# Fewer warm-up products, an earlier LayerNorm tile, and a later weight load on another queue, in a gated mix of linear attention and an MLP mixer

## The chip, the cores and the metric

One core of one Trainium2 chip. The metric is the device time of one execution in microseconds (us), lower is better. "Span" is the time from the first to the last instruction of a profiled execution; it is mostly about 1.7 us shorter than that execution's device time (264.9 against 266.56 us for the profiled run of the kernel before).

Engines by their names in the profile: PE (TensorE matmul), PEld (its weight loads), DVE (VectorE), ACT (ScalarE), POOL (GpSimd), SP (SyncE, used here only to issue DMAs). All times inside an execution count from the start of its span. PE writes its products into PSUM banks (`pp` in the profile); "evacuation" is the copy of a result out of PSUM by another engine. The "clock record" is the trace's list of the stretches in which PE was granted full or half rate.

## The reference, cut to what matters

The input x has 2048 rows of 640. The kernel computes `g*a + (1-g)*b`: g is a sigmoid gate, a is a linear attention with 32 heads of 20, b is a mixer block with two LayerNorms.

```python
def _A_ref(x, wqkv, wo):
    ...                                   # q, k, v per head; phi(t) = t+1 if t > 0 else exp(t), + 1e-6
    kv  = jnp.einsum("bhsd,bhse->bhde", pk, v)
    z   = jnp.einsum("bhsd->bhd", pk)
    num = jnp.einsum("bhqd,bhde->bhqe", pq, kv)
    den = jnp.einsum("bhqd,bhd->bhq", pq, z)[..., None] + 1e-6
    return (num / den) ... @ wo

def _B_ref(x, w1, w2, w3, w4):
    h  = _gelu(_layernorm(x) @ w1)        # LN1
    hs = (four column groups of h, each shifted by 1 or 2 rows) @ w2
    x1 = x + hs
    return x1 + _gelu(_layernorm(x1) @ w3) @ w4      # LN2
```

## The kernel before

Tiles of 512 rows (four) are worked on in chunks of 128 rows (sixteen). The order on each engine is the order of the source text. All PSUM results go through one pool of four pairs of banks, taken in turn.

The start: x's first chunk is loaded and transposed on PE; the other chunks come transposed by DMA. PE is kept busy with products of ones until data is there.

```python
    warmup(6)                # 6 products of 512 columns
    warmup(3, P)             # 3 of 128 columns
    ...                      # 5 PE transposes of x's first chunk (L211), 1 of the gate vector
    warmup(3, P)
    for dc in range(DC):     # 5 slices of the contraction
        k_mm(kp, 0, (dc,))   # K of chunk 0 (L190), 2 products
        if dc < DC - 1:
            warmup(1, 2 * P)
    k_evac(kp, 0)
    for c in range(1, NCH):  # K of chunks 1 to 15
        ...
```

The middle. `ln1_apply(c)` normalises a chunk on DVE into one of four buffers and has the SP queue transpose it by DMA into `lnxT`:

```python
    def ln1_apply(c):
        ...
        lnx = work.tile([P, D], BF16, name="ln")              # pool "work": bufs=4
        nc.vector.tensor_scalar(lnx[:], x_sb[:, c, 0:D], ...) # L297
        nc.sync.dma_start_transpose(lnxT[t][...], lnx[:])     # L299

    def den_evac(pt):        # 1 / den
        nc.scalar.activation(pt[:, 1, :], pt[:, 0, :], ACT.Copy, bias=1e-6)
        ...
            nc.vector.reciprocal(r_bf[:], pt[:, 1, :])        # L254, reads a PSUM pair

    ...
    for cc in range(CPT):
        ln1_apply(2 * CPT + cc)            # LN1 tile 2
    ...
    for fcs in w1_split:
        w1_unit(0, fcs)
    kv_unit()
    den_evac(den_mm())
    for fcs in w1_split:
        w1_unit(1, fcs)
    for cc in range(CPT):
        ln1_apply(3 * CPT + cc)            # LN1 tile 3, the last
    s1.close()
    ...
    nc.gpsimd.dma_start(w4_sb[:, 0:FF, :], ...)      # w4, 2080 KB, and two pieces of 80 KB
    nc.gpsimd.dma_start(w4_sb[0:FR, FF, :], ...)
    nc.gpsimd.dma_start(w4_sb[FR:P, FF, :], ...)
    ...
    for j in range(DC):
        m_unit(j)            # five output-weight units on PE (L379), each copied out by ACT (L381)
    r_unit()                 # spreads the reciprocals over the rows (L259)
    ...                      # W2 (L415), LN2 of tile 0, w1_unit(2), w1_unit(3), then W3 and W4 by tile
```

## Time and profile before

| | before |
|---|---|
| device time, median (range) of the first four runs | 267.24 us (266.69 to 267.68) |
| span of the profiled execution | 264.9 us |
| PE busy | 260.5 us |
| first PE product, first K product, first K product of chunk 1 | 0.83, 4.83, 7.20 us |
| first W2 product | 88.28 us |
| start of the last PE product, and from there to the end | 261.13 us, 3.73 us |

The page of the kernel before, its line of busy times and the head of its chain of waits:

```profile
...
PE 260.5 (98%) x1744; PEld 162.6 (61%) x1744; DVE 139.6 (53%) x270; ACT 84.3 (32%) x122; POOL 22.7 (9%) x58
...
PE 97%; ACT 1%; DVE 0%; issue 0%
...
```

PE is busy practically all of the time and is the chain. So engines other than PE matter only where PE waits for them, and by the start times of PE's products there is just one such place of any size: around `r_unit`, ahead of the first W2 product, the starts are 467 ns apart, where other products of 512 columns, as the row-broadcast's are, follow each other after 216.

The start, from the timeline (start in us, length in us, engine, line, what, count, and in brackets the idle time before it and what ended it):

```profile
...
0.83 3.04 PE L202 MATMUL pp<-const-bfloat16-1.0 128*128 128x512 bf16 x9 [0.83 <-PEq L574]
...
3.67 0.42 PE L211 MATMUL pp<-ident,x_sb 128*128 128x128 bf16 x2
...
4.83 0.74 PE L190 MATMUL pp<-wk_sb,xT 128*128 128x320 bf16 x2
...
5.58 0.64 PE L190 MATMUL pp<-wk_sb,xT 128*128 128x320 bf16 x2
...
6.16 0.44 PE L190 MATMUL pp<-wk_sb,xT 128*128 128x320 bf16 x2
...
```

PE begins at half rate: two K products at 4.83 and 5.09 start 267 ns apart, later ones 136. The trace's clock record has full rate from 5.99 us on. x's first chunk landed at 3.10 us, but nine warm-ups stand ahead of its transposes.

The middle, from the timeline:

```profile
...
78.98 1.39 POOL L396 DMA_DIRECT2D w_sb<-in_B_w_dram  x1 [5.29 <-PE pp L360]
...
80.25 3.36 DVE L254 RECIPROCAL r_bf<-pp 128x512 bf16<-128x512 f32 x1
...
84.97 2.90 PE L379 MATMUL pp<-wo_sb,kvT 128*32 128x320 bf16 x80
...
85.74 3.08 ACT L381 CAST m_sb<-pp 128x640 bf16<-128x640 f32 x5
86.92 1.16 DVE L297 TENSOR_SCALAR ln<-x_sb,mv,rstd 128x640 bf16<-128x640 bf16 x3
...
87.80 0.40 PE L259 MATMUL pp<-r_bf,emat 32*128 32x512 bf16 x4
...
88.28 5.59 PE L415 MATMUL pp<-w_sb,hsT 128*128 128x320 bf16 x40
88.28 0.45 DVE L297 TENSOR_SCALAR ln<-x_sb,mv,rstd 128x640 bf16<-128x640 bf16 x1 [0.20 <-DMA lnxT<-ln]
...
```

The reciprocal (L254) runs directly behind the kv evacuation (the copies into `kvT`, which end at 80.19 us). w4's load is issued from POOL at 78.98 us. The last LN1 tile is normalised (L297, 3 + 1) at 86.9 to 88.7 us, and the fourth of these waits for a transpose: its buffer still held LN1 tile 2, whose fourth transpose was issued at 79.58 us. That one, by source line:

```profile
...
L299 SPq DMA_TRANSPOSE lnxT<-ln x1: 1227/1227/1227, 79.6 to 79.6; - x1
...
DMA to landing us min/median/max: 8.6/8.6/8.6
```

It took 8.6 us from issue to landing; lone ones take 2.6. In that time w4's 2240 KB were on the way.

### The profile page before, as it was taken

The numbers are of one execution on the slowest core, as the hardware profiler recorded it, in microseconds if no ns is written. First come the engines' busy times: TensorE is split into PE (matmuls) and PEld (weight loads), VectorE is DVE, ScalarE is ACT, GpSimd is POOL, SyncE is SP. The second block draws the span as 40 slices with busy tenths as digits, with TensorE's granted clock in tenths as the row PEclk, the third lists the DMA queues.
The fourth block names the chain that finished last, engine by engine and source line by source line (L and its number), as shares of the span: only waits on it lengthen the run. The fifth ranks groups of instructions, "written<-read, shape, count | busy, mean of one in ns | idle before, by whom it ended". The sixth has DMA issues, their size and how long they took to land.

```text
span 264.9 us, 4267 instructions
## 1 busy us (share of the span) xinstructions
PE 260.5 (98%) x1744; PEld 162.6 (61%) x1744; DVE 139.6 (53%) x270; ACT 84.3 (32%) x122; POOL 22.7 (9%) x58
## 2 busy tenths in 40 slices
PE   8999999999999999999999999999999999999994
PEld 4777555788754644555666556567555566455663
DVE  1688778899856797955412364503464413122132
ACT  1555544321165635622420313330222340333100
POOL 7100010012223140001000001000001000000000
PEclk9999999999999999999999999999999999999999
DMA  7999989015668952000132000042000042000011
GB/s 194 148 182 350 369 293 330 9 33 121 125 97 217 228 105 52 0 0 2 25 74 77 25 0 2 11 88 77 25 0 2 1 99 74 27 0 2 0 50 50
DMA packets 44749, 23.62 MB, mean 89 GB/s; under 512 B 35450, under 2 KB 43642, under 8 KB 44730
## 3 DMA queue, kind: packets, MB, share of 16 engines
q1 hardware_dynamic: 43792, 20.57, 32.6%
q0 software_dynamic: 496, 2.29, 2.9%
q10 hardware_dynamic: 442, 0.49, 0.5%
q8 instruction: 13, 0.21, 0.3%
q14 instruction: 6, 0.05, 0.1%
HBM read 12.21 MB, written 2.62 MB: 56 GB/s over the span
## 4 chain that ended last, share of the span: by engine, by line
PE 97%; ACT 1%; DVE 0%; issue 0%
PE pp L479 22%; PE pp L462 21%; PE pp L190 8%; PE pp L307 8%; PE pp L415 8%; PE pp L446 8%; PE pp L341 8%; PE pp L232 8%; PE pp L202 2%; PE pp L467 1%; PE pp L488 1%; ACT m_sb L381 1%; PE pp L360 1%; PE pp L247 0%; PE pp L379 0%; PE pp L211 0%
## 5 line engine op out<-in xcount | busy, mean ns | idle before, releaser
L470 ACT ACTIVATE h<-pp 128x1024 bf16<-128x1024 f32 (+1 forms) x28 | 27.8, 993 | 102.8 <-PE pp L462 94.4
L462 PE MATMUL pp<-lnxT,w_sb 128*128 128x512 bf16 x260 | 60.4, 379 | 0.0
L479 PE MATMUL pp<-w_sb,h 128*128 128x320 bf16 x416 | 57.9, 299 | 0.0
L479 PEld LDWEIGHTS <-h 128*128 128x128 bf16 x416 | 40.0, 98 | 17.0 <-issue 1.9
L462 PEld LDWEIGHTS <-w_sb 128*128 128x128 bf16 x260 | 25.5, 98 | 26.7
L495 DVE SCALAR_TENSOR_TENSOR oc<-pp,omg,x 128x640 bf16<-128x640 f32 x15 | 12.9, 882 | 44.0 <-PE pp L488 27.1
L449 DVE SCALAR_TENSOR_TENSOR x<-pp,gate,x 128x640 f32<-128x640 f32 x16 | 13.9, 868 | 29.4 <-PE pp L446 29.4
L182 ACT ACTIVATE e<-pp 128x640 bf16<-128x640 f32 (+1 forms) x26 | 21.5, 827 | 9.6 <-PE pp L232 9.6
L446 PE MATMUL pp<-m_sb,pqT 128*128 128x320 bf16 x160 | 24.3, 299 | 0.0
L418 DVE TENSOR_TENSOR x<-pp,x_sb 128x640 f32<-128x640 f32 x16 | 13.1, 820 | 20.7 <-PE pp L415 20.7
L415 PE MATMUL pp<-w_sb,hsT 128*128 128x320 bf16 x160 | 23.9, 299 | 0.1
L190 PE MATMUL pp<-wk_sb,xT 128*128 128x320 bf16 (+1 forms) x160 | 23.0, 303 | 0.0
L307 PE MATMUL pp<-x_sb,pk 128*128 128x320 bf16 (+1 forms) x160 | 22.3, 300 | 0.0
L232 PE MATMUL pp<-xT,hsT 128*128 128x512 bf16 x100 | 21.7, 379 | 0.0
L307 PEld LDWEIGHTS <-pk 128*128 128x128 bf16 x160 | 18.8, 117 | 3.5
L415 PEld LDWEIGHTS <-hsT 128*128 128x128 bf16 x160 | 15.6, 98 | 8.2 <-issue 0.2
L446 PEld LDWEIGHTS <-pqT 128*128 128x128 bf16 x160 | 15.7, 98 | 7.7
L190 PEld LDWEIGHTS <-xT 128*128 128x128 bf16 x160 | 15.8, 99 | 6.1
L341 PE MATMUL pp<-lnxT,w_sb 128*128 128x512 bf16 x80 | 17.9, 379 | 0.0
L232 PEld LDWEIGHTS <-hsT 128*128 128x128 bf16 x100 | 11.8, 118 | 9.7
L277 POOL TENSOR_SCALAR rstd<-mv 128x4 f32<-128x4 f32 (+1 forms) x11 | 3.5, 318 | 147.5 <-DVE mv L283 147.5
L184 DVE SCALAR_TENSOR_TENSOR pk<-pp,e 128x640 bf16<-128x640 f32 x16 | 13.2, 825 | 1.7
(79 smaller groups left out, 192.9 us busy)
## 6 DMA issues: line engine op xcount, KB each, us to landing
out_dram<-oc SPq DMA_DIRECT2D x15, 160.0 KB, 1.8
w_sb<-in_B_w_dram SPq DMA_DIRECT2D x1, 2160.0 KB, 8.5
w_sb<-in_B_w_dram POOLq DMA_DIRECT2D x1, 2080.0 KB, 12.7
x_sb<-in_A_x_dram SPq DMA_DIRECT2D x2, 640.0 KB, 9.8
x_sb<-in_A_x_dram SPq DMA_DIRECT2D x1, 1120.0 KB, 8.5
wo_sb<-in_A_wo_dram SPq DMA_DIRECT2D x6, 160.0 KB, 9.2
hsT<-in_A_wqkv_dram SPq DMA_DIRECT2D x1, 800.0 KB, 6.0
m_sb<-in_A_wqkv_dram SPq DMA_DIRECT2D x1, 800.0 KB, 11.0
```

Source lines behind the costliest of these rows:

```text
L182: nc.scalar.activation(ev, src, ACT.Exp)
L184: nc.vector.scalar_tensor_tensor(dst, src, 0.0, ev, op0=ALU.max, op1=ALU.add)
L190: nc.tensor.matmul(pt[:, hf, 0:n], lhsT=xT[:, dc, c * P:(c + 1) * P], rhs=wk_sb[:, dc, hf * HD:hf * HD + n], start=(dc == 0), stop=(dc == ...
L232: nc.tensor.matmul(pt[:, t % 2, :], lhsT=wq_sb[:, dc, :].rearrange("p (m j) -> p j m", j=DC)[:, j], rhs=xT[:, dc, t * TS:(t + 1) * TS], st ...
L307: nc.tensor.matmul(pt[:, hf, 0:HD + hf], lhsT=w, rhs=x_sb[:, c, hf * HD:(hf + 1) * HD + hf], start=(c == 0), stop=(c == NCH - 1))
L341: nc.tensor.matmul(pt[:, i, :], lhsT=w, rhs=lnxT[t][:, dc, :], start=(dc == 0), stop=(dc == DC - 1))
L415: nc.tensor.matmul(pt[:, hf, 0:HD], lhsT=hsT[:, fc, 2 + c * P:2 + (c + 1) * P], rhs=w2_sb[:, fc, hf * HD:(hf + 1) * HD], start=(fc == 0), ...
L446: nc.tensor.matmul(pt[:, hf, 0:HD], lhsT=pqT[:, j, c * P:(c + 1) * P], rhs=m_sb[:, j, hf * HD:(hf + 1) * HD], start=(j == 0), stop=(j == D ...
L449: nc.vector.scalar_tensor_tensor(x1, pt[:, :, 0:HD], gate[:, c:c + 1], x1, op0=ALU.mult, op1=ALU.add)
L462: nc.tensor.matmul(pt[:, k, :], lhsT=w3_sb[:, dc, fc * P:(fc + 1) * P], rhs=lnT[:, dc, :], start=(dc == 0), stop=(dc == DC - 1))
L470: nc.scalar.activation(h2[:, 2 * i * TS:2 * i * TS + n], pt[:].rearrange("p h e -> p (h e)")[:, 0:n], ACT.Gelu_apprx_tanh)
L479: nc.tensor.matmul(dst, lhsT=st[t]["h2"][:, fc * TS + cc * P:fc * TS + (cc + 1) * P], rhs=w4_sb[:, fc, a:b], start=start and fc == 0, stop ...
```

## The change

Intent: let x's first chunk have its turn as soon as it has landed (part 1); put the normalisation of the last LN1 tile ahead of the reciprocal of den (part 2); and take w4's load out of the way of the transposes, onto the SP queue behind LN2 of tile 0 (part 3).

```diff
@@ part 1
-    def k_mm(pt, c, dcs, hfs=(0, 1), last=DC - 1):
+    def k_mm(pt, c, dcs, first=0):
...                                          (start flag on dc == first)
-    warmup(6)
-    warmup(3, P)
+    warmup(5)
+    warmup(1, P)
...
-    warmup(3, P)
-    for dc in range(DC):
-        k_mm(kp, 0, (dc,))
-        if dc < DC - 1:
+    warmup(5, P)
+    for n, dc in enumerate((1, 0, 2, 3, 4)):
+        k_mm(kp, 0, (dc,), first=1)
+        if n < DC - 1:
             warmup(1, 2 * P)
@@ part 2
     kv_unit()
+    for cc in range(CPT):
+        ln1_apply(3 * CPT + cc)
     den_evac(den_mm())
     for fcs in w1_split:
         w1_unit(1, fcs)
-    for cc in range(CPT):
-        ln1_apply(3 * CPT + cc)
     s1.close()
@@ part 3
-    nc.gpsimd.dma_start(w4_sb[:, 0:FF, :], ...)      (and the two small pieces)
...
     for fcs in w1_split:
         w1_unit(2, fcs)
         if fcs[0] == 0:
             ln2_apply(0, CPT - 1)
+    nc.sync.dma_start(w4_sb[:, 0:FF, :], ...)        (and the two small pieces)
     scale_t(0)
```

More of the change, by code (lines that the diff above doesn't have):

```diff
@@ L184, in phi @@
         nc.vector.scalar_tensor_tensor(dst, src, 0.0, ev, op0=ALU.max, op1=ALU.add)
-    def k_mm(pt, c, dcs, hfs=(0, 1), last=DC - 1):
+    def k_mm(pt, c, dcs, first=0):
         for dc in dcs:
-            for hf in hfs:
+            for hf in range(2):
                 n = HD + hf
                 nc.tensor.matmul(pt[:, hf, 0:n], lhsT=xT[:, dc, c * P:(c + 1) * P],
-                                 rhs=wk_sb[:, dc, hf * HD:hf * HD + n], start=(dc == 0), stop=(dc == last))
+                                 rhs=wk_sb[:, dc, hf * HD:hf * HD + n], start=(dc == first), stop=(dc == DC - 1))
     def k_evac(pt, c):
@@ L395 @@
     w4_sb = w4p.tile([P, FF + 1, D], BF16)
-    nc.gpsimd.dma_start(w4_sb[:, 0:FF, :], B_w4[0:FF * P, :].rearrange("(c p) f -> p c f", p=P))
-    nc.gpsimd.dma_start(w4_sb[0:FR, FF, :], B_w4[FF * P:F, :])
-    nc.gpsimd.dma_start(w4_sb[FR:P, FF, :], B_w4[FF * P:F, :])
     h2p = ctx.enter_context(tc.tile_pool(name="h2p", bufs=1))
@@ L538 @@
             ln2_apply(0, CPT - 1)
+    nc.sync.dma_start(w4_sb[:, 0:FF, :], B_w4[0:FF * P, :].rearrange("(c p) f -> p c f", p=P))
+    nc.sync.dma_start(w4_sb[0:FR, FF, :], B_w4[FF * P:F, :])
+    nc.sync.dma_start(w4_sb[FR:P, FF, :], B_w4[FF * P:F, :])
     scale_t(0)
```

## The prediction

> **What bounds the kernel.** TensorE. Page section 1: PE busy 260.5 of 264.9 us; the chain of waits is 97% PE. By start times PE pauses only for 0.83 us at the start, about 0.3 us near 88 us, and 3.4 us after the last product. Only work removed from PE's queue, or PE's waits, can count.
>
> **Part 1, warm-ups.** PE runs at half rate first: 512-column warm-ups start 427 ns apart, and 320-column products go from 267 to 136 ns apart at about 6.0 us. The Trainium skill ("TensorE: Matmul & The Clock Gate", Part 1) says that the clock is released by time of activity, not by a count of products; so I take the release to stay at 6.0 us. x's first chunk lands at 3.10 us but its transposes start at 3.67, behind nine warm-ups (timeline). With six (five of 427 ns, one of 107) PE is free at 3.03, so transposes start at about 3.15. Two more 128-column warm-ups give back 0.2, so the first K product starts at about 4.5 instead of 4.83. Wk rows 1 land at 4.36, so taking them first is safe. These 0.3 us fall in half-rate time, so are worth about 0.15 us: chunk 1's K products start at 7.05, not 7.20. More is capped: the transposed x of chunks 8-11 lands at 16.54 us, its first product starts at 16.73.
>
> **Part 2, last LN1 tile ahead of den.** Four normalisations of 0.39 to 0.45 us now stand on DVE before the 3.36 us reciprocal (now 80.25 to 83.61). They need the four buffers whose transposes are in flight: the second lands at 80.02, the third at 80.87 (an instruction fetch at 77.0 holds these up), and the fourth, issued at 79.58, at 88.19 because w4's load is in its way. Without w4 I expect 2.6 us, so 82.2. Then the fourth normalisation runs at 82.3 to 82.7, the reciprocal to about 86.1. The second output-weight unit takes the PSUM pair that the reciprocal reads; it starts at 85.52 today, so PE waits about 0.6 us, and the first W2 product moves by about 0.5 us through ScalarE's five evacuations. If the fourth transpose lands by 81.3, the reciprocal ends by 85.3 and nothing is lost. Late landing at three in four: +0.4 us. LN1 tile 3, transposed at about 88 instead of 95.2, is needed only at 99: no gain.
>
> **Part 3, w4 on the SP queue.** It leaves POOL (2.5 us of issuing) and the stretch 81 to 92 us, where it slowed transposes whose readers came only at 93.7 and 99.1: no gain. It is issued at about 102, behind the last LN2 transpose; a 2160 KB load took 8.5 us, so it lands near 112; first use 130.2. Worth 0.
>
> **Sum.** 267.38 - 0.15 + 0.4, rounded down for an early landing: 267.5 us; 8 in 10 from 266.8 to 268.2. Faster by 2%: 0.01; within: 0.98; slower: 0.01.
>
> **What would show it.** x transposes at about 3.15, first K product 4.5, chunk 1 7.05; a wait of the fourth normalisation on a transpose; the reciprocal ending at 85 to 86; idle PE ahead of the second output-weight unit; w4 landing before 115; no PE wait after 90 us.
>
> **What would make it wrong.** The clock released at another time (some 0.3 us per run); the instruction fetch missing the transposes, which removes the loss; x's transposed chunks landing later and making the K stretch wait; w4's packets delaying the last LN2 transpose, whose slack is about 1.5 us.

## More of the kernel before

The experiments ran in three sets of rounds on different chips, each with the kernel before in the same rounds.

## The result, and the profile after

| | before | after |
|---|---|---|
| device time, median of 4 runs (range) | 267.24 us (266.69 to 267.68) | 267.70 us (267.51 to 267.72) |
| span of the profiled execution | 264.9 us | 266.0 us |
| clock at full rate from | 5.99 us | 6.76 us |
| first K product, chunk 1's first K product | 4.83, 7.20 us | 4.44, 7.38 us |
| reciprocal ends | 83.61 us | 86.24 us |
| first W2 product | 88.28 us | 89.00 us |
| last PE product starts, and from there to the end | 261.13, 3.73 us | 261.86, 4.15 us |

The ratio of the two is 1.0017, with a 95% interval from 0.9997 to 1.0037: the same within what these runs can tell. (A ratio is the mean time of one kernel's runs over that of the other's of the same rounds, so not quite the ratio of the medians quoted.) The time lies in the predicted range.

The spans differ by 1.15 us, though, and the trace shows where each piece of it lies. The page after:

```profile
...
PE 260.9 (98%) x1743; PEld 162.8 (61%) x1743; DVE 139.4 (52%) x270; ACT 84.3 (32%) x122; POOL 20.3 (8%) x55
...
PE 95%; DVE 2%; DMA 1%; issue 0%; DVEq 0%
...
```

DVE and a DMA have entered the chain. The start:

```profile
...
0.83 2.40 PE L202 MATMUL pp<-const-bfloat16-1.0 128*128 128x512 bf16 x6 [0.83 <-PEq L574]
...
3.09 0.40 PE L211 MATMUL pp<-ident,x_sb 128*128 128x128 bf16 x2
...
4.44 0.74 PE L190 MATMUL pp<-wk_sb,xT 128*128 128x320 bf16 x2
...
5.94 0.74 PE L190 MATMUL pp<-wk_sb,xT 128*128 128x320 bf16 x2
...
6.69 0.48 PE L190 MATMUL pp<-wk_sb,xT 128*128 128x320 bf16 x2
...
```

The transposes start at 3.09 instead of 3.67 us, the first K product at 4.44 instead of 4.83, as wanted. But full rate came 0.77 us later (6.76 against 5.99), so chunk 1 started 0.18 us later, not earlier.

The middle:

```profile
...
80.28 1.36 DVE L297 TENSOR_SCALAR ln<-x_sb,mv,rstd 128x640 bf16<-128x640 bf16 x3
...
82.52 0.45 DVE L297 TENSOR_SCALAR ln<-x_sb,mv,rstd 128x640 bf16<-128x640 bf16 x1 [0.88 <-DMA lnxT<-ln]
82.88 3.35 DVE L254 RECIPROCAL r_bf<-pp 128x512 bf16<-128x512 f32 x1
...
85.15 0.73 PE L379 MATMUL pp<-wo_sb,kvT 128*32 128x320 bf16 x16
...
86.29 2.36 PE L379 MATMUL pp<-wo_sb,kvT 128*32 128x320 bf16 x64 [0.42 <-DVE r_bf L254]
...
88.58 0.40 PE L259 MATMUL pp<-r_bf,emat 32*128 32x512 bf16 x4
...
89.00 3.28 PE L412 MATMUL pp<-w_sb,hsT 128*128 128x320 bf16 x23
...
```

Three normalisations run directly behind the kv evacuation, the fourth waits 0.88 us for its transpose, and the reciprocal (L254) is therefore done at 86.24. PE does the first output-weight unit at 85.15 and then stands idle until 86.29: the second unit takes the PSUM pair that the reciprocal reads. The waits of PE name it:

```profile
...
PE pp L379 <- DVE r_bf L254: 0.4, 1, 0.4
```

The page's idle time (0.42 us) counts from the modelled end of the product before; between the starts are 717 ns, where the kernel before has 126. From the first output-weight product to the first W2 product it is 3.85 us, against 3.31 before: 0.54 us lost. The fourth transpose itself, with w4 out of its way:

```profile
...
L299 SPq DMA_TRANSPOSE lnxT<-ln x1: 1227/1227/1227, 79.8 to 79.8; - x1
...
DMA to landing us min/median/max: 2.6/2.6/2.6
```

From the first W2 product to the last product both kernels take 172.86 us, to the hundredth. w4 landed at 112.31 us, its first use is near 131. The last difference lies behind the last product: 4.15 against 3.73 us to the end, of which 0.35 lie ahead of POOL's last drain, whose start stands 0.39 us behind the end of POOL's instruction before it (0.04 in the kernel before). These instructions are in the trace itself; no view of the profile prints them.

So the 1.15 us are: later full rate about 0.38 (half of 0.77, since work at half rate loses half its time), earlier K about -0.20, PE's wait 0.54, the closing stretch 0.42.

### The profile page after: what moved, and what is told of

Same layout as the page of the kernel before. It is cut to its first block, busy times and chain, and to the rows that moved or that the text cites. A ratio compares the mean times of both kernels' runs of the same rounds, so it can differ in the third digit from the quotient of the medians.

```text
span 266.0 us, 4258 instructions
## 1 busy us (share of the span) xinstructions
PE 260.9 (98%) x1743; PEld 162.8 (61%) x1743; DVE 139.4 (52%) x270; ACT 84.3 (32%) x122; POOL 20.3 (8%) x55
## 4 chain that ended last, share of the span: by engine, by line
PE 95%; DVE 2%; DMA 1%; issue 0%; DVEq 0%
PE pp L476 22%; PE pp L459 21%; PE pp L190 8%; PE pp L307 8%; PE pp L412 8%; PE pp L443 8%; PE pp L232 8%; PE pp L341 6%; PE pp L202 1%; DVE r_bf L254 1%; PE pp L464 1%; DMA lnxT<-ln 1%; PE pp L485 1%; PE pp L379 1%; DVE hsT L351 0%; PE pp L360 0%
## 5 line engine op out<-in xcount | busy, mean ns | idle before, releaser
L183 DVE TENSOR_SCALAR e<-e 128x640 bf16<-128x640 bf16 (+1 forms) x26 | 9.5, 367 | 9.4 <-ACT e L182 7.8
```

## The experiments

Twelve kernels, all with correct results. Each time is a median of that kernel's runs (four to six; two in experiment 4), beside the kernel before in the same rounds (11 runs, 266.71 to 266.92 us). The changed kernel itself was timed only in its own four runs, so it is compared with the others by their ratios to the kernel before.

**1. Part 1 alone, part 2 alone, part 3 alone, and the change without part 2.** Their edits are the parts of the diff above.

Part 1 alone: 

> Part 1 alone on the kernel before. My theory: the clock is released on a grid of 3.413 us that doesn't follow the program (in the two traces full clock lasts 259.41 us = 76 such steps), so the release in this profile may fall anywhere between 4.2 and 7.7 us; the first K product starts at 4.4 to 4.5 us, and chunk 1's first K product lies 0.1 to 0.2 us earlier than it would with the old start at the same release. Median within 0.3 us of before, about 0.15 below. Rival: six warm-ups instead of nine, and the pause before the transposes, put the release off by themselves (5.99 to 6.76 us between the two traces): release again near 6.7 us, chunk 1 again at about 7.4, time about 0.2 us above before. No wait at the second output-weight unit in either.

Measured: 266.60 us against 266.92, ratio 0.9989 (0.9971 to 1.0007). Full rate from 5.64 us, first K product 4.45, chunk 1 at 6.83. The gain of 0.3 us is twice the expected 0.15, and within the noise. The release was neither near 6.7 nor was chunk 1 near 7.4: the rival falls. That the release follows a grid of its own, whatever the start, is seen when the profiles are put side by side (here the eight in which chunk 1 hardly waited for its data; in part 3 alone it started 0.06 us behind the landing of its own transposed x, which may be why that row's last number is 4.27):

| start of the kernel | full rate from | chunk 1's first K product | the latter minus half the former |
|---|---|---|---|
| old (before, part 2 alone, part 3 alone) | 5.99, 5.18, 4.51 us | 7.20, 6.80, 6.52 us | 4.21, 4.21, 4.27 us |
| new (after, part 1 alone, change without part 2, exp. 2 first, exp. 3 first) | 6.76, 5.64, 6.71, 6.33, 6.75 us | 7.38, 6.83, 7.34, 7.17, 7.39 us | 4.00, 4.01, 3.99, 4.01, 4.02 us |

Within each start the release scatters over more than a microsecond, chunk 1 moves by half of it, and the two starts differ by 0.20 us or a little more: that is what part 1 is worth. (Five more profiles with the new start's order have a release between 4.16 and 5.30 us and chunk 1 at 6.53 to 6.72 us, 0.04 to 0.16 us behind the landing of its own transposed x, so there the rule breaks off.) Full rate lasted 259.41 us in twelve of the fourteen, which is 76 x 3.413 us. In experiment 4 it lasted 262.83 us, which is 77 such steps, and in part 2 alone 85.33 and 177.49 us (25 and 52 steps) around a stretch of half rate of 3.41 us (one step). So the step comes out of these traces by themselves. In the thirteen profiles with warm-ups the release came 3.3 to 5.9 us after PE's first product, never less than about one step. The Trainium skill ("TensorE: Matmul & The Clock Gate", Part 1) states a free-running window of 3413 ns, and that the transition therefore depends on where in the window the first product lands; these traces agree.

Where full rate comes early the 0.20 us don't arrive, or not all of them. With release at 4.51 us: part 1 undone (part 3 alone), chunk 1 at 6.52 us; part 1 in place (exp. 3, second kernel), 6.71 us, both held by data that had not landed. Chunk 8 needs a DMA-transposed piece of x, and in seven of the fourteen profiles its first product starts within 0.06 us of that landing: for instance part 1 alone, landed 16.39, started 16.44 us, and part 3 alone, 16.16 and 16.21.

Part 2 alone, w4 still loaded from POOL: 

> Part 2 alone: the last LN1 tile ahead of den, but w4 still loaded from POOL at about 79 us. My theory (the fourth normalisation waits for the buffer whose transpose w4's load holds up until 88.2 us, and the reciprocal and the PSUM pair wait behind it): the fourth normalisation at about 88.3, the reciprocal ends at about 92.1, PE idle about 6.5 us ahead of the second output-weight unit, time about 273.9 us. Rival (the four normalisations cost only their own 1.7 us of DVE ahead of the reciprocal, and the pause in the changed kernel is that): reciprocal ends at 85.3, no more than 0.3 us lost, 267.3 us.

Measured: 273.46 us against 266.92, ratio 1.0251 (1.0224 to 1.0278). The timeline:

```profile
...
87.36 0.45 DVE L297 TENSOR_SCALAR ln<-x_sb,mv,rstd 128x640 bf16<-128x640 bf16 x1 [6.06 <-DMA lnxT<-ln]
87.72 3.35 DVE L254 RECIPROCAL r_bf<-pp 128x512 bf16<-128x512 f32 x1
...
91.13 3.71 PE L379 MATMUL pp<-wo_sb,kvT 128*32 128x320 bf16 x64 [5.58 <-DVE r_bf L254]
...
95.09 1.13 PE L415 MATMUL pp<-w_sb,hsT 128*128 128x320 bf16 x7
...
```

The fourth normalisation waited 6.06 us for its transpose (issued at 79.44, landed at 87.26 us), the reciprocal ended at 91.07, and PE stood idle 5.58 us for the pair. The chain from w4's load through the buffer and the PSUM pair to PE is shown, and with it why the change moves w4: part 2 without part 3 costs 6.5 us. The page's row of PE's granted clock shows a cost that I had not expected here:

```profile
...
PEclk9999999999999799999999999999999999999999
...
```

In the fourteenth slice the clock fell to half rate, by the clock record from 90.51 to 93.93 us. The Trainium skill (the same page, "Why this matters for your kernels") warns of idle gaps over about 3 us; this pause of 5.58 us did it, and pauses of 0.3 to 1.1 us in other runs did not. The half rate adds about 1.2 us: from the first output-weight product to W2 the kernel lost 6.96 us (10.27 against 3.31), of which the pause makes 5.75. So the expected time of 273.9 us was met in part by luck: the pause was shorter than the expected 6.5 us, and the half rate filled the difference.

Part 3 alone: 

> Part 3 alone: w4 loaded behind LN2 of tile 0 on the SP queue. My theory: off the chain, so same as before within 0.2 us (267.3); the fourth transpose of LN1 tile 2 lands near 82.3 instead of 88.2, w4 lands near 112, first used at 130, and no new PE pause. Rival: w4's move costs something by itself, in the last LN2 transpose or in the closing stretch (the changed kernel's span has 0.4 us more after its last product, with a gap before POOL's last drain): then 0.3 to 0.5 us above before.

Measured: 266.91 us against 266.92, ratio 0.9998 (0.9983 to 1.0012). The fourth transpose landed at 81.56, w4 at 110.90 us, no new PE pause. But the closing stretch was 4.14 us, as in the changed kernel. So part 3 is not free in the profile; the timed runs show no loss, and their interval ends at +0.3 us. Each timed run is listed with its span, though, and there part 3 alone is longer (mean 265.20 against 264.93 us); what hides it is time outside the span, in these rounds 1.99 us on average for the kernel before and 1.70 with part 3.

The change without part 2: 

> The changed kernel with part 2 undone (parts 1 and 3 stay). My theory: the pause of 0.6 us ahead of the second output-weight unit is the only steady loss of the change, so it goes and the time is about 0.5 us below the changed kernel, 267.1 to 267.2 us; reciprocal ends at about 83.7. Rival: the loss sits in the start (clock released later) or in the closing stretch: then it stays at 267.6 to 267.7.

Measured: 267.14 us against 266.92, ratio 1.0005 (0.9991 to 1.0018); the pause is gone (126 ns between starts), 3.31 us from the first output-weight product to W2, closing stretch 4.14 us. Beside the changed kernel's 1.0017 that is 0.3 us less, where 0.5 was expected; the intervals of the two overlap. Both theories had a share: the pause is one steady loss, the closing stretch another. The comparison that isolates part 3 best lies in the same rounds: this kernel and part 1 alone differ by part 3 only, and their runs average 267.09 and 266.67 us. That is 0.42 us, the size of the closing stretch, but six runs each leave it uncertain by some 0.5 us.

**2. Which link holds PE.** Both on the changed kernel.

```diff
-    work = ctx.enter_context(tc.tile_pool(name="work", bufs=4))
+    work = ctx.enter_context(tc.tile_pool(name="work", bufs=8))
```

> The changed kernel with eight buffers for the normalised tiles instead of four, so the four early normalisations have no transpose to wait for. My theory (the wait for the fourth buffer, 0.88 us in the changed kernel, is what pushes the reciprocal past the moment at which PE wants its PSUM pair): the four run back to back, the reciprocal ends about 5.2 us after the kv evacuation instead of 6.0, before the second output-weight unit's turn, so PE's pause there (717 ns between starts) is gone, and the time is that of the kernel with part 2 undone, about 0.5 us below the changed kernel. Rival (the 1.7 us of DVE work is itself enough to make PE wait): a pause of 0.3 us or more stays.

Measured: 267.00 us against 266.71, ratio 1.0006 (0.9992 to 1.0021). The timeline:

```profile
...
80.08 1.50 DVE L297 TENSOR_SCALAR ln<-x_sb,mv,rstd 128x640 bf16<-128x640 bf16 x4
81.50 3.35 DVE L254 RECIPROCAL r_bf<-pp 128x512 bf16<-128x512 f32 x1
...
84.94 2.90 PE L379 MATMUL pp<-wo_sb,kvT 128*32 128x320 bf16 x80
...
```

All four normalisations run together, the reciprocal ends at 84.85, and the eighty output-weight products run through. The four normalisations as DVE work cost PE nothing; the wait for the buffer did. This one was timed 0.3 us below the changed kernel's ratio, again less than the 0.5 of the traces, within the noise.

```diff
-        nc.scalar.activation(pt[:, 1, :], pt[:, 0, :], ACT.Copy, bias=1e-6)
+        dn = den_p.tile([P, TS], F32, name="dn")          # an SBUF tile
+        nc.scalar.activation(dn[:], pt[:, 0, :], ACT.Copy, bias=1e-6)
-            nc.vector.reciprocal(r_bf[:], pt[:, 1, :])
+            nc.vector.reciprocal(r_bf[:], dn[:])
```

> The changed kernel with ScalarE's copy of den going to an SBUF tile and the reciprocal reading that, so that the PSUM pair is free after ScalarE's copy. The fourth normalisation still waits for its transpose and the reciprocal still ends as late as in the changed kernel (about 6.0 us after the kv evacuation). My theory: PE waited for the pair alone, so the pause ahead of the second output-weight unit goes, although the reciprocal is as late; the first W2 product comes about 0.55 us earlier relative to the first output-weight product (3.31 instead of 3.85 us); time about 0.5 us below the changed kernel. Rival (the late reciprocal also holds PE by its result, or through the copies of hx behind it): 0.3 us or more of pause stays, at the row-broadcast or the first W2 product.

Measured: 267.00 us against 266.71, ratio 1.0009 (0.9994 to 1.0024). The timeline (line numbers are two higher here):

```profile
...
81.84 0.45 DVE L299 TENSOR_SCALAR ln<-x_sb,mv,rstd 128x640 bf16<-128x640 bf16 x1 [0.90 <-DMA lnxT<-ln]
82.21 3.35 DVE L256 RECIPROCAL r_bf<-dn 128x512 bf16<-128x512 f32 x1
...
84.53 2.90 PE L381 MATMUL pp<-wo_sb,kvT 128*32 128x320 bf16 x80
...
87.84 2.33 PE L414 MATMUL pp<-w_sb,hsT 128*128 128x320 bf16 x16
...
```

The fourth normalisation still waits 0.90 us and the reciprocal still ends 5.81 us after the kv evacuation (5.87 in the changed kernel), but PE runs through, and W2 follows 3.31 us after the first output-weight product. So the late reciprocal held PE through the PSUM pair alone.

**3. The closing stretch.** Both on the changed kernel.

```diff
     nc.gpsimd.memset(kvT[:], 0.0)
+    for _ in range(8):
+        nc.gpsimd.memset(mhalf[:], -0.5)      # the value it has already
```

> The changed kernel with eight tiny extra instructions on POOL near its start, as many as POOL lost with w4's three loads (79 recorded instructions against 71). In all three profiles with w4 on SP the stretch from the last product's start to the end is 4.15 us, in all three with w4 on POOL 3.70 to 3.73; the 0.4 us lie ahead of POOL's last drain, and an instruction fetch appears at the end. Theory A (POOL's instruction stream ends just behind a fetch boundary, which the shorter stream brings to the exposed end): closing stretch 3.7 us again. Theory B (what counts is that no load goes out on POOL's queue): it stays 4.15. The pause of 717 ns stays in both.

Measured: closing stretch 3.65 us; 267.23 us against 266.71, ratio 1.0012 (0.9997 to 1.0027); the pause stayed (779 ns).

```diff
-    nc.sync.dma_start(w4_sb[FR:P, FF, :], B_w4[FF * P:F, :])
+    nc.gpsimd.dma_start(w4_sb[FR:P, FF, :], B_w4[FF * P:F, :])
```

> The changed kernel with only the last 80 KB piece of w4 issued from POOL, at the same place of the program. Theory B (a load on POOL's queue is what shortens the end): closing stretch 3.7 us. Theory A (number of POOL instructions): one load adds two or three of the eight missing instructions, so it depends on where the boundary lies; if the stretch is 4.15, B is out. The pause of 717 ns stays in both; time that of the changed kernel or 0.4 us less.

Measured: closing stretch 3.73 us; 266.99 us against 266.71, ratio 1.0009 (0.9995 to 1.0023); a pause of 589 ns. POOL has 77 recorded instructions here.

Theory B falls with the eight memsets, which put nothing on POOL's queue and still shorten the end. Theory A agrees with both: with 71 POOL instructions the end is 4.09 to 4.15 us in seven profiles, with 77 or 79 it is 3.64 to 3.73 in seven (those of part 6 below included). With 71 an instruction fetch of 8192 bytes stands at the very end of all seven traces; with 77 or 79 that last one is gone, and there is one more earlier (at 74.3 us with the memsets). That POOL waits for that fetch is not shown: its record begins 0.3 to 0.6 us after the end of the span, too late for the gap. What is shown is that the number of POOL's instructions decides it: the eight memsets are the only difference between 4.15 and 3.65 us.

**4. The instruction fetch that holds up transposes.** On the changed kernel:

```diff
-    warmup(5)
-    warmup(1, P)
+    for i in range(75):
+        nc.tensor.matmul(warm[0:32, 1, 0:32], lhsT=one[:, 0:32], rhs=one[:, 0:32], start=True, stop=True)
```

> The changed kernel with its six first warm-ups replaced by 75 tiny ones (32 x 32), which puts 138 more instructions on PE's stream, so that PE's instruction fetches fall at other places: in place of the one at 76.4 to 77.6 us (in all ten traces so far) one near 66 and one near 83 us are expected. In all ten traces the transpose of LN1 tile 2 that is issued at about 76 us lands 3.9 to 4.1 us after its issue, and lone ones elsewhere 2.6. My theory (the fetch holds the transposes up, so also the fourth, so also the fourth normalisation): with no fetch near 77 us they land 2.6 us after issue, or at most a few tenths more; the fourth lands near 81.3, the fourth normalisation waits little or not, and PE's pause ahead of the second output-weight unit is at most 0.2 us. Rival (the transposes are slow there for another reason, or the fetch only coincides): 3.9 us and the pause stay. The start may be later by up to 2 us, and tells nothing here.

Measured: the fetches came at 65.44 and 80.45 us, so the second did not get clear of the transposes as planned. By source line, the one issued at 76.7 and the one issued at 78.1 us:

```profile
...
L299 SPq DMA_TRANSPOSE lnxT<-ln x1: 1227/1227/1227, 76.7 to 76.7; - x1
...
DMA to landing us min/median/max: 2.6/2.6/2.6
```

```profile
...
L299 SPq DMA_TRANSPOSE lnxT<-ln x1: 1227/1227/1227, 78.1 to 78.1; - x1
...
DMA to landing us min/median/max: 4.4/4.4/4.4
```

The second of the tile, slow in every earlier trace, took 2.6 us; the third, in flight at 80.45 us, took 4.4 and the fourth 3.7. The one in flight at 65.44 us took 3.54 us (issued 65.04, landed 68.58), the others around it 2.6 to 2.7. So a slow transpose goes where the fetch goes, and the rival falls. All fourteen traces together say the same: after 50 us, 362 transposes that met neither a PE fetch (16,384 bytes) nor a load took 2.4 to 2.7 us, and of 49 that a fetch met, without a load beside them, 43 took 2.9 to 4.4 us. The other six took 2.6; they met the fetch in their last 0.3 us or were issued more than 0.5 us after its start. My number for the pause missed, since the fetch still hit: the third normalisation waited 1.29 us and the pause grew to 1358 ns. How large the pause is thus depends on where PE's instruction stream happens to be refilled. Device time 268.56 us (two runs), of no use for the question.

**5. No warm-ups at all.** On the changed kernel, every `warmup` call taken out.

> The changed kernel with no warm-up product at all. My theory (full clock comes at the end of the first whole 3.413 us step of the free-running grid in which PE was busy; the first step of the traced starts, with PE idle for its first quarter or more, never sufficed): PE starts at 3.1 us, so the release falls between 6.5 and 9.9 us instead of 4.2 to 7.6, the first chunk's K products wait for the weights (landed 4.2 to 5.9), and the time is about 0.9 us above the changed kernel's. Rival (warm-ups hardly matter, since x and the weights come late anyhow): within 0.3 us of the changed kernel.

Measured: 269.49 us against 266.83, ratio 1.0092 (1.0077 to 1.0108), some 2.0 us above the changed kernel (1.0092 - 1.0017, times 267). Full rate from 9.73 us, inside the expected stretch. The size was off by a factor of two: in the trace the last product starts 1.82 us later than in the changed kernel, of which 1.21 us arose up to the last K product and 0.61 in the pause, which is 1321 ns here; PE's stream is shorter, and a fetch at 60.10 us fell into the row of LN1 transposes: the SP queue issued its next one 2.01 us later instead of 1.35. Against the changed kernel all later transposes are 1.8 to 1.9 us late, up to the fourth of tile 2, which lands at 84.25 us, while PE's products ahead of the pause are 1.21 us late. Warm-ups do matter; having three fewer ahead of the transposes did not show in the timed runs.

**6. Both losses undone, and one step further.** The changed kernel with eight buffers and the eight memsets:

> The changed kernel with both of its losses undone: eight buffers for the normalised tiles, and eight tiny instructions on POOL. If the losses add up (0.55 us of pause and 0.42 us of closing stretch in the traces), it has neither the pause nor the longer end, and stands at 0.2 us below before, the worth of part 1 alone: about as the kernel with part 1 alone (0.3 below before in its rounds). Rival (the closing stretch is an effect of profiling only): it stands at 0.2 above before like the one with eight buffers.

Measured: 266.70 us against 266.83, ratio 0.9999 (0.9985 to 1.0013); no pause (125 ns), closing stretch 3.66 us, full rate from 5.30 us. In the trace both losses are gone together. This kernel's timed runs stand between theory (-0.2 us) and rival (+0.2) and can't choose. More runs lean to the theory: over the kernels with the new start and no long pause, the 18 runs with 71 POOL instructions (the change without part 2 and both of experiment 2) average 267.04 us and the 12 with 79 (part 1 alone and this one) 266.71, which is 0.33 us apart (95% interval about 0.03 to 0.63; chosen afterwards, from three sets of rounds).

The same with one copy moved:

```diff
-        nc.scalar.copy(m_sb[:, j, :].rearrange("p (h e) -> p h e", h=2), pt[:, :, 0:HD])
+        copy = nc.vector.tensor_copy if j == 2 else nc.scalar.copy
+        copy(m_sb[:, j, :].rearrange("p (h e) -> p h e", h=2), pt[:, :, 0:HD])
```

> The same with the third of the five output-weight copies on DVE instead of ScalarE, to shorten ScalarE's row of five copies, behind which the first W2 product waits (467 ns between starts in every trace without the long pause). Theory: the step from the row-broadcast to the first W2 product shrinks by about 0.2 us, time about 0.2 us below the kernel with both losses undone. Rival (PE waits there for something else, or DVE's copy comes too late behind the copies of hx): no change.

Measured: 266.57 us against 266.83, ratio 0.9988 (0.9975 to 1.0001). The timeline:

```profile
...
86.70 0.82 DVE L384 CAST m_sb<-pp 128x640 bf16<-128x640 f32 x1
87.15 1.29 ACT L384 CAST m_sb<-pp 128x640 bf16<-128x640 f32 x2 [0.34 <-PE pp L381]
...
87.58 0.40 PE L261 MATMUL pp<-r_bf,emat 32*128 32x512 bf16 x4
...
87.90 2.35 PE L415 MATMUL pp<-w_sb,hsT 128*128 128x320 bf16 x16
...
```

DVE's copy (86.70) runs beside ScalarE's, which now waits 0.34 us for PE instead of PE for it; from the row-broadcast to W2 it is 0.32 us instead of 0.47, and from the first output-weight product to W2 3.16 instead of 3.31. It has the lowest median of its rounds, 0.26 us below the kernel before, with an interval that still touches 1.

## Why the prediction was right, point by point

- **The bound.** Right: from the first W2 product on nothing but PE's own work counts, 172.86 us in both kernels.
- **Part 2, "+0.4 us".** Right, step by step: fourth transpose 82.2 predicted, 82.42 measured; fourth normalisation 82.3 to 82.7 against 82.52 to 82.97; reciprocal 86.1 against 86.24; PE's wait 0.6 us against 0.59 (717 - 126 ns); W2 0.5 us later against 0.54. Shown by the two experiments that cut the chain at the buffer and at the pair, and by part 2 alone, which stretched it to 5.58 us.
- **The instruction fetch as the reason for late transposes.** Right; shown where it was moved.
- **Part 1, "about 0.15 us".** The worth was about right where full rate came late, 0.20 us at equal release of the clock; where it came early, x's transposed chunks capped it. The step that failed is "I take the release to stay at 6.0 us": it lay between 4.16 and 6.76 us in the thirteen profiles with warm-ups, and in the profiled execution after it ate the gain twice over (0.38 us). The free-running window told of above already spoke against it. I named this among the things that could go wrong, with 0.3 us; it should have been in the sum as a spread on both kernels. The cap by chunk 8's landing was right.
- **Part 3, "Worth 0".** Wrong. w4's arrival was right (112 us; 112.31), and no PE wait followed. But the closing stretch grew by 0.42 us in every profile with 71 POOL instructions. I looked only for what the moved load would wait for or hold up, not at what a shorter POOL stream does at the end of the program.
- **The sum.** Predicted +0.1 us, medians +0.46, interval from -0.1 to +1.0 us. By the traces the effects are -0.20 + 0.54 + 0.42 = +0.76 us, or a little more where the landing of x eats the 0.20; that is inside the interval. The sum left out 0.42 us, and its range, 1.4 us wide, absorbed them. It also holds the median of the kernel before (267.24), so a hit by itself says little; the evidence is in the steps of part 2. What stays open: how much of the 0.42 us the timed runs contain. Part 3 alone, timed, shows none of it (at most +0.3); part 3 on top of part 1 shows 0.42, and the larger set of runs in experiment 6 shows 0.33, both with wide intervals.

## What to carry to other kernels

Before moving work ahead of something on an engine, look up which buffer it writes and when the last reader of that buffer, here a DMA, is done: 1.7 us of DVE work was free, and a wait of 0.88 us for its fourth buffer cost PE 0.54. Two parts of a change can depend on each other in one direction: part 2 without part 3 costs 6.5 us, and part 3 without part 2 only the longer end of the program (0.4 us in the traces). Where effects are tenths of a microsecond and the clock's release alone moves a run by more, read them from start times in several traces, at equal release, rather than from the medians.

## What the Trainium skill lacked or had wrong

- "Runtime: NRT & Kernel Launch", section "Instruction fetch mechanics", describes a refill in 16 KiB blocks and calls its cost "mostly hidden". The 16,384-byte fetches are in these traces, but they are not hidden from other DMAs: of the DMA transposes that met a fetch 43 of 49 took 2.9 to 4.4 us instead of 2.4 to 2.7, and through a buffer that reached PE. No page that I found says that fetches slow transposes.
- The same section has nothing on the end of a program: with eight POOL instructions fewer (71 instead of 79 recorded) the stretch behind the last product was 4.1 instead of 3.7 us. The cause behind the count is open.
- "DMA: Bandwidth & Descriptors", section "Issuing engines are not separate DMA queues", says that DMAs of all engines interleave on the same 16 engines, and these traces agree. It gives no size for it: a transpose of 160 KB on the SP queue took 8.6 us beside 2240 KB issued from POOL, 2.6 us without.
- "TensorE: Matmul & The Clock Gate", Part 1, gives the scatter of the transition as about 500 ns either way. Here it lay anywhere from 4.16 to 6.76 us with the first product at 0.83 us, a range of 2.6 us; the free-running window of 3413 ns on the same page is the better guide.
